# Gate rows of a fused attention and expert kernel: constant rows filled in place, the first two pairs' rows copied from SBUF, two pairs' q and k in flight

## The chip, the cores and the metric

The kernel runs on one core of one Trainium2 chip. The metric is the time of one launch in device microseconds, the median of the runs shown; before the change it is 846.34 us.

## The reference

Three stages follow each other: causal attention with a cumulative gate, and two feed-forward layers. Only the first is touched by the change.

```python
cum = np.cumsum(np.maximum(s, 0.0), axis=-1)           # s: 4 x 8 x 576
bias = -(cum[:, :, :, None] - cum[:, :, None, :])
scores = scale * q @ k.T                               # q, k, v: 4 x 8 x 576 x 64
scores = np.where(causal, -1e9, scores + np.minimum(bias, 0.0))
attn = softmax(scores); x = attn @ v
...
h = x @ w_in; h = layer_norm(h * softmax(h)) * g_ln; x = h @ w_out
h = x @ w2_in; out = (h * clip(h + 3, 0, 6) / 6) @ w2_out
```

Below the diagonal the bias is never positive, so the minimum leaves it as it is. A score is thus q.k plus cum of the key minus cum of the query, and the kernel lets the matrix engine add these two terms.

## The kernel before

The 32 heads are worked in 16 pairs. Pairs 0 to 3 are the first batch, and their scores are computed by `qk_whole` in two matmuls of 64 rows each: one contracts the head's 64 dimensions (tile `HL`, or the first half of tile `whole`), the other contracts the gate rows in the second half of `whole`. `whole` has four planes of 576 columns. Planes 2 and 3 hold, for each head of the pair, 64 rows of which four count: on one side ones and the negated sums, on the other side the sums and ones, with each sum split into a high and a low part. The rows behind the four must not contribute. There are two `whole` tiles, for even and odd pairs; pairs 2 and 3 use them again.

`gate_rows` makes these rows for all heads. It loads s, clips it, scans it into `cum`, splits that into `pos`, and negates it into `neg` (L278 to L282, on VectorE). Four DMAs (L286) write ones, `pos` and `neg` to the DRAM table `rows_d`. `load_gates` (L427) reads a pair's rows back from it, one DMA for each head. GpSimd fills planes 2 and 3 of both tiles with zeros beforehand (L290).

`load_qk` loads q and k of a pair in four DMAs (L395) into a ring of two tiles. So q and k of pair 1 can only be loaded when TensorE has transposed those of pair 0 (L440), which ScalarE and VectorE then evict (L445, L447).

Behind the scores come the maxima (L531, VectorE), the exponentials (L543, ScalarE), the reciprocal sums (L639, L640), the normalising (L644, GpSimd), the transposes of the probabilities (L678) and the product with v (L707). The weights w_in come in eight pieces of 512 KB on ScalarE's DMA queue (L317) into a ring of two and are decoded by ScalarE, VectorE and GpSimd (L323 to L347); the first expert matmuls (L812) stand behind the pairs.

The order of all work is made by a planner, `Plan`. Each step is added with its engine, an assumed duration, what it reads and writes and which ring it takes. `emit` then plays the steps through: every engine takes the ready step that was added first, and the instructions are issued in that order. Each engine runs its instructions strictly in order. A DMA counts on one of eight shared counters when it lands, and waits for the DMA before it on the same counter; the order shows the counters as DMAHW0 to DMAHW7.

The plan's start reads:

```python
    gate_rows()
    load_qk(0)
    for name in "qk":
        prep_qk(0, name)
    load_qk(1)
    load_v(0, 0)
```

## Time and profile before

| | before |
|---|---|
| median of 3 runs | 846.34 us (845.79 to 846.7) |
| profiled execution | 846.22 us, its span 844.4 us |
| TensorE (PE) busy | 818.4 us, 97% of the span |
| VectorE (DVE) busy | 438.5 us, 52% |
| ScalarE (ACT) busy | 399.4 us, 47% |
| GpSimd (POOL) busy | 209.4 us, 25% |
| mean granted TensorE clock | 0.994 |

The span runs from the first to the last instruction that the profile shows; the launch adds 1.8 us around it. SPq and ACTq are the instruction queues of SyncE and ScalarE where they issue DMAs. A busy TensorE is not TensorE at its best, since the granted clock has two levels, 1.2 and 2.4 GHz; it is shown as a share of the higher one.

### The profile page before, as it was taken

To read this page: it belongs to the slowest core of one execution; us is meant where nothing else is said; L and a number is where in the kernel's file an instruction comes from. 1 tells how busy PE (TensorE), PEld (TensorE's weight loads), DVE (VectorE), ACT (ScalarE), POOL (GpSimd) and SP (SyncE) were. 2 spreads that over 40 slices of the span, in tenths; PEclk is the share of its full clock that TensorE was granted. 3 is DMA by queue.
4 is the path that set the end of the run, shared out by engine and by line. 5 is a ranking of instruction groups with operands and counts; after the bars stand their busy time and mean duration, and the time that the engine had idled before them with its cause. 6 is when DMAs were issued, how large, how long until landed. Compare 5 with 4: busy or idle time off the path is not lost.

```text
span 844.4 us, 13546 instructions
## 1 busy us (share of the span) xinstructions
PE 818.4 (97%) x4864; PEld 689.5 (82%) x4864; DVE 438.5 (52%) x1125; ACT 399.4 (47%) x928; POOL 209.4 (25%) x309
## 2 busy tenths in 40 slices
PE   4899999999999999999999999999999999999997
PEld 3565588898898889888999999998888888888886
DVE  4677887746855574749826982234222322222221
ACT  2575767755765575736636662244222422232222
POOL 1563643424632363327402220000000000000000
PEclk9899999999999999999999999999999999999999
DMA  6753596755646455223605640012000300010001
GB/s 172 180 152 110 120 209 152 176 120 130 129 118 137 98 129 120 65 99 121 193 32 194 214 148 1 1 62 88 1 1 0 100 1 0 1 50 1 0 1 50
DMA packets 95938, 77.52 MB, mean 92 GB/s; under 512 B 64288, under 2 KB 78112, under 8 KB 95872
## 3 DMA queue, kind: packets, MB, share of 16 engines
q1 hardware_dynamic: 93568, 68.27, 31.9%
q10 hardware_dynamic: 2304, 8.39, 3.1%
q8 instruction: 38, 0.62, 0.3%
q14 instruction: 28, 0.23, 0.1%
HBM read 45.38 MB, written 10.03 MB: 66 GB/s over the span
## 4 chain that ended last, share of the span: by engine, by line
PE 91%; DVE 4%; DMA 1%; POOL 1%; issue 1%; ACT 0%; POOLq 0%; DVEq 0%; SPq 0%; ACTq 0%
PE bank L1071 24%; PE bank L1102 24%; PE bank L899 11%; PE bank L812 11%; PE bank L707 6%; PE bank L678 5%; PE bank L610 5%; PE bank L583 3%; PE bank L878 2%; PE bank L473 1%; DMA stack<-HL12k 1%; DVE y L531 0%; DMA rows_d<-neg 0%; POOL y L626 0%; POOL y L644 0%
## 5 line engine op out<-in xcount | busy, mean ns | idle before, releaser
L1071 PE MATMUL bank<-x2h,w 128*128 128x512 f32 (+1 forms) x640 | 185.3, 370 | 0.0
L1102 PE MATMUL bank<-w,gh 128*128 128x512 f32 x576 | 178.8, 393 | 0.0
L1079 DVE SCALAR_TENSOR_TENSOR g<-g,bank 128x512 f32<-128x512 f32 (+1 forms) x80 | 50.6, 633 | 206.3 <-ACT g L1075 206.0
L1071 PEld LDWEIGHTS bank<-x2h,w 128*128 128x128 f32 x640 | 118.7, 188 | 18.7
L1075 ACT ACTIVATE g<-bank 128x512 f32<-128x512 f32 (+1 forms) x80 | 44.5, 556 | 178.8 <-PE bank L1071 178.7
L1102 PEld LDWEIGHTS bank<-w,gh 128*128 128x128 f32 x576 | 107.9, 188 | 21.9
L1071 PE MATMUL bank<-x2l,w 128*128 128x512 f32 (+1 forms) x320 | 118.5, 370 | 0.0
L1102 PE MATMUL bank<-w,gl 128*128 128x512 f32 x288 | 111.9, 391 | 0.0
L531 DVE CUSTOM_DVE_ANT_0 y<-bank,mask 96x288 f32<-96x288 f32 (+4 forms) x168 | 74.6, 467 | 57.3 <-PE bank L610 37.7
L543 ACT ACTIVATE y<-y,nmax 128x256 f32<-128x256 f32 (+4 forms) x140 | 83.4, 597 | 41.4 <-DVE nmax L531 29.9
L626 POOL TENSOR_SCALAR y<-y,rsum 128x128 f32<-128x128 f32 (+4 forms) x120 | 68.1, 589 | 103.7 <-DVE rsum L622 48.5
L899 PE MATMUL bank<-zh,w_out_h 128*128 128x256 f32 x288 | 82.8, 288 | 0.0
L899 PE MATMUL bank<-zl,w_out_h 128*128 128x256 f32 x288 | 81.2, 282 | 0.0
L899 PE MATMUL bank<-zh,w_out_l 128*128 128x256 f32 x288 | 81.2, 282 | 0.0
L1087 DVE TENSOR_TENSOR gl<-g,gh 128x512 fp32r<-128x512 f32 (+1 forms) x80 | 53.7, 671 | 43.4 <-ACT gh L1083 42.6
L1083 ACT CAST gh<-g 128x512 fp32r<-128x512 f32 (+1 forms) x80 | 46.2, 577 | 48.2 <-DVE g L1079 48.1
L1071 PEld LDWEIGHTS bank<-x2l,w 128*128 128x128 f32 x320 | 60.0, 188 | 8.3
L1102 PEld LDWEIGHTS bank<-w,gl 128*128 128x128 f32 x288 | 54.1, 188 | 12.1
L812 PE MATMUL bank<-w_in_h,xh 128*128 128x512 f32 x144 | 61.6, 428 | 0.8 <-DVE xh L794 0.8
L610 PE MATMUL bank<-stack 128*96 128x288 f32 (+4 forms) x288 | 57.8, 317 | 1.2 <-DMA stack<-HL12k 0.8
L812 PE MATMUL bank<-w_in_h,xl 128*128 128x512 f32 x144 | 57.4, 399 | 0.6 <-POOL xl L798 0.6
L812 PE MATMUL bank<-w_in_l,xh 128*128 128x512 f32 x144 | 57.4, 398 | 0.0
(220 smaller groups left out, 1360.9 us busy)
## 6 DMA issues: line engine op xcount, KB each, us to landing
raw_w2i<-in_moe_w_in_dram SPq DMA_DIRECT2D x16, 512.0 KB
raw_w2o<-in_moe_w_out_dram SPq DMA_DIRECT2D x16, 512.0 KB
rawq<-in_q_dram SPq DMA_DIRECT2D x32, 144.0 KB
rawk<-in_k_dram SPq DMA_DIRECT2D x32, 144.0 KB
x_d<-x2s SPq DMA_DIRECT2D x36, 128.0 KB
out_dram<-ob SPq DMA_DIRECT2D x18, 256.0 KB
raw_wi<-in_moe_w_in_dram ACTq DMA_DIRECT2D x8, 512.0 KB
raw_wo<-in_moe_w_out_dram ACTq DMA_DIRECT2D x8, 512.0 KB
```

What stands on the lines that cost most here:

```text
L531: nc.vector.tensor_tensor_reduce(out=ys[h, t][:n, c0:c1], in0=bank(key)[:n, : c1 - c0], in1=mask[:n, 480 + n - w + c0 : 480 + n - w + c1], ...
L543: nc.scalar.activation(out=y[:n], in_=y[:n], func=AF.Exp, bias=nmax[:n, h, t : t + 1], scale=-1.0, accum_out=sums[:n, h, t : t + 1])
L610: nc.tensor.matmul(bank(key)[:n, : c1 - c0], lhsT=ss[:, 2 - 2 * m, ST[t] : w], rhs=ss[:, 3 - 2 * m, c0:c1], start=(m == 0), stop=(m == 1))
L626: nc.gpsimd.tensor_scalar(ys[h, t][:n], ys[h, t][:n], rsum[:n, h, t : t + 1], 1.0, ALU.mult, ALU.mult)
L707: nc.tensor.matmul(bank(key)[j * D : (j + 1) * D, lo - c0 : c1 - c0], lhsT=vs[v_key(p, a)][:n, jj, j, :], rhs=pts[pt_key(2 * p + j, a)][:n ...
L812: nc.tensor.matmul(bank(key), lhsT=xs[i][m // 2][:, kk, :], rhs=(w_in_l if m == 1 else w_in_h)[:, kk, f * 512 : (f + 1) * 512], start=(kk ...
L899: nc.tensor.matmul(bank(key)[:, : 2 * P], lhsT=w_out_at(w, kk)[:, m * P : (m + 1) * P], rhs=z[:, kk, :], start=(kk == 0 and i == 0), stop= ...
L1071: nc.tensor.matmul(bank(key)[:, :w], lhsT=wt[:, a, 0, c * P : (c + 1) * P], rhs=x[:, c, :w], start=(c == 0 and i == 0), stop=(c == KDM - 1 ...
L1079: nc.vector.scalar_tensor_tensor(out=gg, in0=gg, scalar=6.0, in1=bank(key)[:, :w], op0=ALU.min, op1=ALU.mult)
L1083: nc.scalar.copy(gh[:, :w], gg[:, :w])
L1087: nc.vector.tensor_sub(gl[:, :w], gg[:, :w], gh[:, :w].bitcast(F32))
L1102: nc.tensor.matmul(bank(key), lhsT=g_t[ci, m][1 + i // 2][:, t * P : (t + 1) * P], rhs=w2[m][:, i % 2, 1, :], start=(m == 0 and i == 0), s ...
```

## The change

The change has three parts.

- Constant rows in place. Instead of zeros, the planes get their constants directly: plane 2 becomes all ones, plane 3 zeros with minus one in the first four rows of each head. The sign moves from the sums to the constant, so `neg` is not made any more, and a row of minus ones (`minus`) takes its place in the table. The fill moves from GpSimd to VectorE and is added first in the plan.
- Gate rows of pairs 0 and 1 straight from SBUF. In the first pass `load_gates` copies the rows out of `pos` into the tile, with two DMAs for each head (`direct`). The writes to `rows_d`, which the later pairs still read, are added behind the loads of pair 1 (`store`).
- Two pairs' q and k at once. q and k of the odd pairs of the first batch go into the two tiles that the first expert layer later uses for its transposed activations (tags zh and zl), and k of pair 0 is loaded on ScalarE's queue. The other edits rename keys.

```diff
@@ -269,7 +269,8 @@
         one = ap2.tile([P, S], F32, tag="y4", name="one")[:NH]
         cum = ap2.tile([P, NQ, 2, D], F32, tag="V", name="cum").rearrange("p c j d -> p (c j d)")[:NH, :S]
         pos = ap2.tile([P, PT_COLS], F32, tag="pt", name="pos", bufs=PT).bitcast(F32R)[:NH, : 2 * S]
-        neg = ap2.tile([P, PT_COLS], F32, tag="pt", name="neg", bufs=PT).bitcast(F32R)[:NH, : 2 * S]
+        minus = ap2.tile([P, PT_COLS], F32, tag="pt", name="minus", bufs=PT)[:NH, :S]
+        once["pos"] = pos
         def load():
             nc.sync.dma_start(out=s_sb, in_=s.rearrange("b h s -> (b h) s"))
...
@@ -279,25 +280,32 @@
             nc.vector.tensor_tensor_scan(cum, one, s_sb, 0.0, ALU.mult, ALU.add)
             nc.vector.tensor_copy(pos[:, :S], cum)
             nc.vector.tensor_sub(pos[:, S:], cum, pos[:, :S].bitcast(F32))
-            nc.vector.tensor_scalar_mul(neg, pos.bitcast(F32), -1.0)
         def put(i, r, src):
             dst = rows_d[:, i, r::2, :]
             nc.sync.dma_start(out=dst, in_=src)
-        def zeros(j):
+        def fixed(j):
             whole_t[j] = ap1.tile([P, 4, S], F32, tag=f"stack{j}", name=f"whole{j}")
-            nc.gpsimd.memset(whole_t[j][:, 2:4, :], 0.0)
-
-        plan.add("SP", 0.45, load, writes=["s"], lag=2.0)
-        plan.add("POOL", 2.2, lambda: nc.gpsimd.memset(one, 1.0), writes=["one"])
+            nc.vector.memset(whole_t[j][:, 2, :], 1.0)
+            nc.vector.memset(whole_t[j][:, 3, :], 0.0)
+            for x in range(2):
+                nc.vector.memset(whole_t[j][x * D : x * D + 4, 3, :], -1.0)
+
+        for j in range(2):
+            plan.add("DVE", 1.2, lambda j=j: fixed(j), writes=[f"zeros{j}"], new=[(f"stack{j}", 1, f"whole{j}")])
+        plan.add("SP", 0.4, load, writes=["s"], lag=2.0)
+        plan.add("POOL", 0.6, lambda: nc.gpsimd.memset(one, 1.0), writes=["one"])
+        plan.add("POOL", 0.6, lambda: nc.gpsimd.memset(minus, -1.0), writes=["minus"])
         plan.add("DVE", 3.0, sums, reads=["s", "one"], writes=["c"])
-        ones = one.unsqueeze(1).to_broadcast([NH, 2, S])
-        both = lambda c: c.bitcast(F32).rearrange("p (i s) -> p i s", i=2)
-        for i, r, src, key in ((1, 0, both(pos), "c"), (0, 1, both(neg), "c"), (0, 0, ones, "one"), (1, 1, ones, "one")):
-            plan.add("SP", 0.55, lambda i=i, r=r, src=src: put(i, r, src), reads=[key], writes=[f"rows/{i}{r}"], lag=2.0)
-        for j in range(2):
-            plan.add("POOL", 1.3, lambda j=j: zeros(j), writes=[f"zeros{j}"], new=[(f"stack{j}", 1, f"whole{j}")])
+        twice = lambda c: c.unsqueeze(1).to_broadcast([NH, 2, S])
+        both = pos.bitcast(F32).rearrange("p (i s) -> p i s", i=2)
+
+        def store():
+            for i, r, src, key in ((1, 0, both, "c"), (0, 1, both, "c"), (0, 0, twice(one), "one"), (1, 1, twice(minus), "minus")):
+                plan.add("SP", 0.55, lambda i=i, r=r, src=src: put(i, r, src), reads=[key], writes=[f"rows/{i}{r}"], lag=2.0)
+
+        once["store"] = store
     def split64(plan, pool, src, hi, lo, name, key, scale=None, bufs=1, ring="", raws64=2, after=(), hi_dve=False, on_dve=(), behind=None, needs=(), home=()):
...
@@ -389,14 +397,20 @@
     def load_qk(p):
         b, hp = divmod(p, NPAIR)
+        spare = p < NPAIR and p % 2 == 1
+
         def rows(name, src):
-            raws[p, name] = ap2.tile([96, 6, 2, D], F32, tag="raw", name=f"raw{name}{p}")
+            if spare:
+                raw = bcp.tile([P, 2 * P * KFF], F32, tag="z" + "hl"["qk".index(name)], name=f"raw{name}{p}", bufs=1)
+                raws[p, name] = raw[:96, : 12 * D].rearrange("p (c j d) -> p c j d", c=6, j=2)
+            else:
+                raws[p, name] = ap2.tile([96, 6, 2, D], F32, tag="raw", name=f"raw{name}{p}")
             for j in range(2):
-                nc.sync.dma_start(out=raws[p, name][:, :, j, :], in_=src[b, 2 * hp + j].rearrange("(c p) d -> p c d", c=6))
+                (nc.scalar if p == 0 and name == "k" else nc.sync).dma_start(out=raws[p, name][:, :, j, :], in_=src[b, 2 * hp + j].rearrange("(c p) d -> p c d", c=6))
         for name, src in (("q", q), ("k", k)):
-            key = f"raw{name}{p}"
-            plan.add("SP", 1.1, lambda name=name, src=src: rows(name, src), writes=[key], new=[("raw", 2, key)], lag=4.0)
+            new = [("raw", 2, f"raw{name}{p}")] if not spare else [("z" + name, 1, f"raw{name}{p}")]
+            plan.add("ACT" if p == 0 and name == "k" else "SP", 1.0, lambda name=name, src=src: rows(name, src), writes=[f"raw{name}{p}"], new=new, lag=4.0)
     def v_key(p, a):
...
@@ -422,16 +436,24 @@
     def load_gates(p, a):
+        def direct():
+            for j in range(2):
+                row = once["pos"].bitcast(F32)[2 * p + j : 2 * p + j + 1, :].rearrange("o (i s) -> o i s", i=2)
+                for i, r in ((0, 1), (1, 0)):
+                    nc.sync.dma_start(out=whole_t[p % 2][j * D + r : j * D + r + 3 : 2, 2 + i, :], in_=row)
+
         def gates():
             for j in range(2):
                 nc.sync.dma_start(out=gates_at(p, j)[:4], in_=rows_d[2 * p + j].rearrange("i r s -> r i s"))
+        if p < 2 and not a:
+            return plan.add("SP", 1.6, direct, reads=["c", f"zeros{p}"], writes=[f"G{p}{a}"], new=[("G", 2, f"G{p}{a}")], lag=2.0)
         plan.add("SP", 0.8, gates, reads=ROWS_D + [f"zeros{p % 2}", f"whole{p % 2}"], writes=[f"G{p}{a}"], new=[("G", 2, f"G{p}{a}")], lag=2.0)
     def prep_whole(p, name):
         n = S // 6
-        i, raw_key, hl_key = "qk".index(name), f"raw{name}{p}", f"HL{p}"
+        i, hl_key = "qk".index(name), f"HL{p}"
         def turn(c0, key):
             if name == "q" and c0 == 0:
...
@@ -886,7 +907,7 @@
                                  zh[:, 4 * f : 4 * f + 4, o : o + P].bitcast(F32))
         first = i % 2 == 0 and f == 0
-        plan.add("PE", 0.43, turn, reads=[f"e{i}/{f}"], writes=[key], new=[("z", 1, f"z{c}")] if first else [], bank=key)
+        plan.add("PE", 0.43, turn, reads=[f"e{i}/{f}"], writes=[key], new=[("zq", 1, f"z{c}"), ("zk", 1, f"zl{c}")] if first else [], bank=key)
         plan.add("ACT", act(512), high, reads=[key], writes=[f"z{c}/h{f}_{i % 2}"])
         plan.add("DVE", dve(512), low, reads=[key, f"z{c}/h{f}_{i % 2}"], writes=[f"z{c}/l{f}_{i % 2}"])
...
@@ -975,6 +996,7 @@
     for name in "qk":
         prep_qk(0, name)
     load_qk(1)
+    once["store"]()
     load_v(0, 0)
     plan.add("SP", 0.5, lambda: nc.sync.dma_start(out=g_sb, in_=g_ln.rearrange("(c p) -> p c", p=P)), writes=["g"], lag=2.0, after=["HL0/k0"])
     for b, share in enumerate(SHARES):
```

On SyncE (SP), the place is the gate rows of the first two pairs. `whole_125` and `whole_134` are the tiles of pairs 0 and 1 before, `whole_117` and `whole_131` after. Before:

```order
L286 DMA rows_d<-pos 32x2x576 [waits DMAHW1_49,DVE_49]
L286 DMA rows_d<-neg 32x2x576 [waits DMAHW2_49,DVE_49]
L395 DMA rawq_147<-in_q_dram 96x6x64 [waits DMAHW3_49,PE_49]
L395 DMA rawq_147<-in_q_dram 96x6x64 [waits DMAHW4_49]
L395 DMA rawk_162<-in_k_dram 96x6x64 [waits DMAHW5_49,PE_49]
L395 DMA rawk_162<-in_k_dram 96x6x64 [waits DMAHW6_49]
L427 DMA whole_125<-rows_d 4x2x576 [waits DMAHW2_49,DMAHW7_49,DMAHW1_49,Pool_49]
L427 DMA whole_125<-rows_d 4x2x576 [waits DMAHW0_49]
L413 DMA V0a<-in_v_dram 128x2x64
L979 DMA g_sb<-in_moe_g_ln_dram 128x8x1
L427 DMA whole_134<-rows_d 4x2x576 [waits DMAHW3_49,Pool_49]
L427 DMA whole_134<-rows_d 4x2x576 [waits DMAHW4_49]
```

After:

```order
L443 DMA whole_117<-pos 2x1x576 [waits DMAHW5_49,DVE_49]
L443 DMA whole_117<-pos 2x1x576 [waits DMAHW6_49]
L443 DMA whole_117<-pos 2x1x576 [waits DMAHW7_49]
L443 DMA whole_117<-pos 2x1x576 [waits DMAHW0_49]
L286 DMA rows_d<-pos 32x2x576 [waits DMAHW1_49]
L286 DMA rows_d<-pos 32x2x576 [waits DMAHW2_49]
L427 DMA V0a<-in_v_dram 128x2x64 [waits DMAHW3_49]
L1001 DMA g_sb<-in_moe_g_ln_dram 128x8x1 [waits DMAHW4_49]
L443 DMA whole_131<-pos 2x1x576 [waits DMAHW5_49]
L443 DMA whole_131<-pos 2x1x576 [waits DMAHW6_49]
L443 DMA whole_131<-pos 2x1x576 [waits DMAHW0_49]
L443 DMA whole_131<-pos 2x1x576 [waits DMAHW1_49]
```

The reads from the table have become four copies for each pair, the writes of `pos` stand between the two pairs' copies, and the loads of v and g_sb stand ahead of pair 1's copies, each with a wait for a counter.

On ScalarE (ACT), the place is the first two w_in loads after the change, which count on the same counters:

```order
L467 ACTIVATE HL_152<-bank_96 128x288 [waits PE_49]
L467 ACTIVATE HL_152<-bank_97 128x288 [waits PE_49]
L325 DMA raw_wi_0_175<-in_moe_w_in_dram 128x1024 [waits DMAHW2_49]
L467 ACTIVATE HL_168<-bank_100 128x288 [waits PE_49]
L467 ACTIVATE HL_168<-bank_101 128x288 [waits PE_49]
L325 DMA raw_wi_0_189<-in_moe_w_in_dram 128x1024 [waits DMAHW4_49]
```

Before, both loads stood directly behind the first two evictions; the second one now stands behind the evictions of pair 1's q.

On VectorE (DVE), the place is the start of the program. Before:

```order
L278 TENSOR_SCALAR s_sb<-s_sb 32x576
L279 SCALAR_TENSOR_TENSOR cum<-one,s_sb 32x576
L280 CAST pos<-cum 32x576
L281 TENSOR_TENSOR pos<-cum,pos 32x576
L282 TENSOR_SCALAR neg<-pos 32x1152
L447 COPY HL_137<-bank_98 128x288
L447 COPY HL_137<-bank_99 128x288
```

After:

```order
L290 MEMSET whole_117 128x576
L291 MEMSET whole_117 128x576
L293 MEMSET whole_117 4x576 x2
L290 MEMSET whole_131 128x576
L291 MEMSET whole_131 128x576
L293 MEMSET whole_131 4x576 x2
L279 TENSOR_SCALAR s_sb<-s_sb 32x576
L280 SCALAR_TENSOR_TENSOR cum<-one,s_sb 32x576
L281 CAST pos<-cum 32x576
L282 TENSOR_TENSOR pos<-cum,pos 32x576
L469 COPY HL_152<-bank_98 128x288
L469 COPY HL_152<-bank_99 128x288
```

Eight memsets stand ahead of the sums, and the negation is gone.

On TensorE (PE), the place is the first scores, behind the transposes of pair 0's q. Before:

```order
L440 MATMUL bank_98<-ident,rawk_122 128x96 x3
L440 MATMUL bank_99<-ident,rawk_122 128x96 x3
L583 MATMUL bank_100<-whole_125 128x128
L583 MATMUL bank_101<-whole_125 128x128
L583 MATMUL bank_100<-HL_137 128x128
L583 MATMUL bank_101<-HL_137 128x128
L440 MATMUL bank_102<-ident,rawq_147 128x96 x3
L440 MATMUL bank_103<-ident,rawq_147 128x96 x3
L583 MATMUL bank_96<-whole_125 128x256
L583 MATMUL bank_97<-whole_125 128x256
```

After:

```order
L462 MATMUL bank_98<-ident,rawk_127 128x96 x3
L462 MATMUL bank_99<-ident,rawk_127 128x96 x3
L462 MATMUL bank_100<-ident,rawq_136 128x96 x3
L462 MATMUL bank_101<-ident,rawq_136 128x96 x3
L462 MATMUL bank_102<-ident,rawk_139 128x96 x3
L462 MATMUL bank_103<-ident,rawk_139 128x96 x3
L605 MATMUL bank_96<-whole_117 128x128
L605 MATMUL bank_97<-whole_117 128x128
L605 MATMUL bank_96<-HL_152 128x128
L605 MATMUL bank_97<-HL_152 128x128
```

The transposes of q and k of pair 1 now stand ahead of pair 0's first scores; before, they stood between the scores.

## Rows read from the trace of the kernel before

**Rows 1.** Part 2 of the page: busy tenths of TensorE in 40 slices.
```profile
PE   4899999999999999999999999999999999999997
```

**Rows 2.** Busy time by stretch: length, then each engine's busy us.
```profile
0.00:10.00 10.00, 2.39 (x12) 1.86 (x12) 6.36 (x7) 2.31 (x4) 4.20 (x13) 1.00 0.65 179
10.00:20.00 10.00, 5.00 (x24) 3.76 (x25) 1.65 (x6) 2.27 (x7) 0.00 (x0) 1.00 0.61 149
```

**Rows 3.** Timeline, gate rows: start, duration, engine; idle before in brackets.
```profile
0.72 0.40 SPq L275 DMA_DIRECT2D s_sb<-in_s_dram  x1
...
2.73 2.04 POOL L290 MEMSET whole<- 128x1152 f32 x2
2.74 2.34 DVE L278 TENSOR_SCALAR s_sb<-s_sb 32x576 f32<-32x576 f32 x1 [2.74 <-DMA s_sb<-in_s_dram]
...
5.19 1.35 DVE L279 TENSOR_TENSOR_SCAN cum<-one,s_sb 32x576 f32<-32x576 f32 x1
...
6.57 0.45 DVE L280 CAST pos<-cum 32x576 fp32r<-32x576 f32 x1
7.06 0.75 DVE L281 TENSOR_TENSOR pos<-cum,pos 32x576 fp32r<-32x576 f32 x1
...
7.84 0.75 DVE L282 TENSOR_SCALAR neg<-pos 32x1152 fp32r<-32x1152 f32 x1
...
12.93 0.60 SPq L427 DMA_DIRECT2D whole<-rows_d  x2
...
15.00 0.93 PE L583 MATMUL bank<-whole 64*128 64x128 f32 x3 [7.93 <-DMA whole<-rows_d]
```

**Rows 4.** Chain of waits, 8 to 15 us: start, duration, what.
```profile
8.61 4.17 DMA rows_d<-neg
12.93 1.93 DMA whole<-rows_d
```

**Rows 5.** Timeline, loads of the first 15 us and their users.
```profile
1.18 0.96 SPq L395 DMA_DIRECT2D rawq<-in_q_dram  x2
...
4.66 1.19 PE L440 MATMUL bank<-ident,rawq 96*128 96x96 f32 x6 [4.66 <-DMA rawq<-in_q_dram]
...
5.90 0.87 ACTq L317 DMA_DIRECT2D raw_wi<-in_moe_w_in_dram  x2
...
10.62 0.68 ACT L323 ACTIVATE a_wi<-raw_wi 128x512 f32<-128x512 f32 x1 [4.32 <-DMA raw_wi<-in_moe_w_in_dram]
...
14.03 0.47 SPq L979 DMA_DIRECT2D g_sb<-in_moe_g_ln_dram  x1
```

**Rows 6.** Busy time by stretch of 2 us, as rows 2.
```profile
24.00:26.00 2.00, 1.02 (x7) 0.66 (x5) 1.72 (x5) 1.32 (x4) 2.00 (x4) 0.90 0.38 82
26.00:28.00 2.00, 2.00 (x11) 1.43 (x9) 0.48 (x2) 1.70 (x6) 1.63 (x2) 0.50 0.64 145
...
56.00:58.00 2.00, 2.00 (x5) 1.64 (x6) 2.00 (x10) 0.93 (x3) 2.00 (x3) 0.58 1.12 299
```

**Rows 7.** Timeline, TensorE's transposes (L440) and scores (L583), 15 to 31 us.
```profile
15.80 0.77 PE L583 MATMUL bank<-HL 64*128 64x128 f32 x3
...
16.50 1.22 PE L440 MATMUL bank<-ident,rawq 96*128 96x96 f32 x6
...
18.67 1.06 PE L583 MATMUL bank<-HL 64*128 64x256 f32 x4
...
20.82 0.80 PE L583 MATMUL bank<-whole 64*128 64x128 f32 x4
...
23.58 0.69 PE L440 MATMUL bank<-ident,rawq 96*128 96x96 f32 x6 [0.55 <-DMA whole<-rows_d]
...
28.03 2.51 PE L583 MATMUL bank<-whole 64*128 64x128 f32 x14
```

**Rows 8.** Timeline, normalising on GpSimd and the transposes behind it.
```profile
23.84 2.55 POOL L644 TENSOR_SCALAR y<-y,rsum 128x128 f32<-128x128 f32 x4 [0.76 <-DVE rsum L640]
...
25.58 1.56 PE L678 MATMUL bank<-ident,y 128*128 128x128 f32 x5 [0.98 <-POOL y L644]
```

More of the change, by code (lines that the diff above doesn't have):

```diff
@@ L454, in prep_whole @@
             key = f"pp{p}{name}{c0}"
-            plan.add("PE", 3 * 0.083, lambda c0=c0, key=key: turn(c0, key), reads=[raw_key, *home], writes=[key],
+            plan.add("PE", 3 * 0.083, lambda c0=c0, key=key: turn(c0, key), reads=[f"raw{name}{p}", *home], writes=[key],
                      new=ring if name == "q" and c0 == 0 else [], bank=key, after=[] if name == "q" and c0 == 0 else [f"pp{p}q0"])
@@ L464, in prep_qk @@
         n = S // 6
-        hl_key, raw_key = f"HL{p}{name}", f"raw{name}{p}"
+        hl_key = f"HL{p}{name}"
         groups = [(0, 6)] if 6 * n <= 512 else [(0, 3), (3, 6)]
@@ L498, in prep_qk @@
             key, m = f"pp{p}{name}{c0}", (c1 - c0) * n
-            plan.add("PE", (c1 - c0) * (0.01 + 0.000833 * n), lambda c0=c0, c1=c1, key=key: turn(c0, c1, key), reads=[raw_key], writes=[key],
+            plan.add("PE", (c1 - c0) * (0.01 + 0.000833 * n), lambda c0=c0, c1=c1, key=key: turn(c0, c1, key), reads=[f"raw{name}{p}"], writes=[key],
                      new=[("HL0", 2, hl_key)] if c0 == 0 else [], bank=key, after=[f"pp{p}{name}0"] if c0 else [])
@@ L766, in pairs @@
             qs = [(0.0013 * (ST[t] + SZ[t]), lambda p=p, t=t: qk_whole(p, t)) for t in ts]
-            k = 0
             for i, x in enumerate(qs):
```

2 lines of the change are left out of this document (1 added, 1 removed).

## The prediction

> **What bounds the kernel now.** I read the page first. TensorE is busy 97% of the span, and of its 40 slices only the first two and the last show less than 9 tenths [rows 1]. So nearly every microsecond of the run is TensorE work, and a change in the first 20 us can save only what TensorE idles there, or does at its lower clock. The busy time by stretch then shows how much that is: 2.4 and 5.0 us busy in the first two stretches of 10 us [rows 2]. What is gained before 60 us should therefore stay gained up to the end, unless a stall is put in somewhere behind. The timeline has the largest hole there: TensorE waits 7.93 us for the gate rows of pair 0, which come back from the DRAM table rows_d [rows 3].
>
> The timeline and the chain of waits show how that hole is made [rows 3, 4]. s_sb arrives at 2.74, but VectorE's first operation on it takes 2.34 us. The cast of the same 576 columns takes 0.45, and GpSimd's memset of `whole` runs from 2.73 to 4.77 beside it. The sums end at 7.81, the negatives at 8.59. Their write to rows_d is issued at 8.61 and takes 4.17 us; the read is issued at 12.93 and takes 1.93; the score matmuls of pair 0 start at 15.00.
>
> **The change, step by step.**
>
> *When `pos` is ready.* VectorE now fills both `whole` tiles itself, ahead of the sums: eight memsets of 576 columns. The trace has no memset on VectorE. Bounds from its nearest rows: 0.45 us each (the cast of 576 columns) and 0.75 (the subtraction of 576 columns); GpSimd's memset, 1.02 for 1152 columns, gives 0.51 [rows 3]. I take 0.6, between the two and near the third. From the start at 0.72 (where the other queues start) the memsets end at 5.5, with bounds 4.3 and 6.7. GpSimd's 2.04 us on `whole` are gone, so the first operation on s_sb should take about 0.45 like the cast, and then come scan, cast and subtraction: 1.35 + 0.49 + 0.78 (start to start) [rows 3]. `pos` is ready at 5.5 + 3.1 = 8.6 (7.4 to 9.8), which is 0.8 later than before. The removed `neg` (0.75) cancels that.
>
> The Trainium skill (VectorE: DVE Perf Modes, section "Zero memsets can be issued as uint32 (trn2)") says that a memset takes one cycle per element whatever the type; at the 0.96 GHz it gives for VectorE that is 0.6 us each, an estimate from that page, and `pos` at 8.6 as well. No row here shows it. On the 2.34 us, the row shows VectorE released 0.3 us after GpSimd's memset ended. The same skill (SBUF — State Buffer, section "Who interferes with whom") says that the two engines share a port pair and the second to issue is blocked; the row agrees, and if the blocking also held for the new memsets, `pos` would come at up to 10 us.
>
> *Pair 0.* No table write lies between `pos` and the copy now. Four copies of 2 rows each are issued on SP, 0.30 us apart (two of the old reads took 0.60) [rows 3]: 8.6, 8.9, 9.2, 9.5. Each should take the 1.93 us of the old read, the same rows in the same number of bytes; the upper bound is the 4.17 of the write [rows 4]. Head 0 is complete at 10.85, head 1 at 11.45.
> Meanwhile TensorE transposes q and k of both pairs. The loads of k of pair 0 go out on ScalarE's queue beside q's, and q of pair 1 right behind on SP. The first transposes start at 4.66 now [rows 5]; with k's 144 KB times two in flight beside q's I put them at 5.2. Six take 1.2 us at this place [rows 5], so all 24 end at 10.0. Pair 0's scores start at 10.85 instead of 15.00, and pair 1's 2.4 us of transposes are already behind.
>
> *Pair 1: the new wait.* Every DMA of the program waits for the one before it on the same of eight counters (the order shows it as DMAHW0 to 7). On SP the small load of g_sb now shares a counter with the second w_in load, which ScalarE issues after q of pair 1 is evicted, at about 9.4 (transposes to 8.8, two evictions). Before, both w_in loads were issued from 5.90 on, and the first was in use at 10.62, 4.72 later [rows 5]. With 4.72 the second lands at 14.1; g_sb's issue takes 0.47 [rows 5]; behind it stand pair 1's four copies, 14.6 to 15.5, the second of which lands at 16.8. So TensorE, done with pair 0 at 10.85 + 1.57 + 2.07 = 14.5 (the durations of the same matmuls: 15.00 to 16.57, 17.66 to 19.73 [rows 7]), has a new idle stretch of about 2.3 us, and pair 1's scores run from 16.8 to 20.4.
>
> *Pair 2.* Behind pair 1's copies, q of pair 2 is issued by 16.7 and, with the 2.5 to 3.5 us of the first q (issued 1.18 and 1.66, in use at 4.66 [rows 5]), is there before 20.4. Its transposes end at 21.6. The transposes of pair 0's probabilities need GpSimd's normalising; before, that ended 11.4 us after pair 0's first score (26.39 against 15.00 [rows 3, 8]), and now VectorE has less between, so it ends by 22.2 at the latest. Five of those six transposes took 1.56 us, so 1.9 for six [rows 8]: 23.5. k of pair 2 adds 1.2: 24.7 with everything at the lower clock.
> The gate rows of pair 2 still come from rows_d. The load of v ahead of them on SP waits for the third w_in load: issued at about 16, landing at 20.7, then 0.5 for the issue, 0.9 for v and two reads, and 1.93: about 23.8 at the latest, just hidden.
> Pair 2's scores began at 28.03 [rows 7].
>
> *TensorE's clock.* The same six transposes take 1.22 at 16.50 and 0.69 at 23.58, so the first ran at the lower level; four of the scores of 128 columns take 0.80 at 20.82, so it was fast by then [rows 7]. In 24 to 26 TensorE was busy 1.02 of 2 us, and in 26 to 28 the granted clock is 0.50, the 1.2 GHz level [rows 6]. So it worked nearly without a gap from 15.00 until it was fast at about 20.8, and after a gap around 24 to 25.5 it was slow again. By the same course it would be fast again about 5.8 us after 16.8, at 22.6, which takes 0.9 off what follows: pair 2 starts at 23.8, 4.2 us earlier. Before, the work from 28.03 to about 32.4 ran at the lower level; at the full one it would take 2.2 less. I count 1.3 of that, since the other engines must follow.
>
> *The sum.* 4.2 + 1.3 = 5.5 us. The rest costs nothing by itself: `minus` (a GpSimd memset of 576 columns) where GpSimd idles, the two extra stores of `pos` behind the copies. The profiled execution took 846.22 us (span 844.4), close to the median 846.34. So 840.7 for a profiled execution and **840.8** for the median.
>
> **Bounds.** If each copy takes 4.17 instead of 1.93, pair 1 starts 2.2 later; without the clock's 1.3 the gain is 2.0: 844.3. If the second w_in load lands in 3 us, pair 1 starts 1.7 earlier; with all 2.2 of the clock and the second slow stretch at 56 to 60 (granted clock 0.58 in its first half [rows 6], so about 1.7 lost) avoided the gain is 4.2 + 1.7 + 2.2 + 1.7 = 9.8: 836.5.
>
> **Rivals.**
> - *Smaller gain* (0.16): copies queue behind the loads and the clock stays low, 843 to 844.5. For it: the write of 4.17. Against it: the read of 1.93, which moved as little as the copies do, while the write moved 144 KB.
> - *Larger gain* (0.12): the upper bound above, 836 to 837.5.
> - *Given back* (0.10): the two w_in loads go out 1 and 3 us later than before; if the first expert matmuls near 56 us wait for the decoded w_in and not for attention, the start is bought for nothing: 846.3. Against it: those loads are paced by attention work on ScalarE, which moves forward too.
> - *Slower* (0.06): v of pair 1 on SP, and with it pair 2's gate rows, wait for the third w_in load. If that lands at 24.7 nothing is gained; if it takes 12 us from its issue at 16, pair 2 starts at about 31.3, 3.3 late: 849.6. Against it: 4.72 for the first with another behind it.
>
> **How the numbers follow.** The likeliest, 0.56, is a gain of 3.5 to 7.5 us. With the smaller and the larger gain the range 836.5 to 844.8 holds a little over 8 in 10. A difference of under 0.2% (1.7 us) can't be told from no change. Faster: 0.56 + 0.12 + most of 0.16, 0.81. Same: the rest of it and most of "given back", 0.12. Slower: 0.07.
>
> **What would show it.** The wait of 7.9 us for rows_d is gone; pair 0's scores start near 10.9; a wait for pair 1's copies of about 2 us stands at 14 to 17; the first operation on s_sb takes under 0.6; pair 2's scores start near 23.8; the granted clock is full at 28 to 32. The prediction is wrong if the memsets take over 1 us each, if SP stands at g_sb beyond 16, or if TensorE idles more than before between 30 and 100 us.

## The result and the profile after

The change made the kernel slower by 4.1 us. The median of six runs is 850.61 us (849.82 to 854.38), against 846.52 (845.79 to 846.92) for six runs of before in the same measurement: a ratio of 1.0057, 95% interval 1.0038 to 1.0076. The profiled execution took 850.73 us (span 849.0), 4.5 more than that of before, so it shows what has to be explained.

Part 2 of the page of after, TensorE's busy tenths:

```profile
PE   5799999999999999999999999999999999999998
```

In [rows 1] the first two slices show 4 and 8 and the last shows 7: the first has gained a tenth, the second has lost one and the last has gained one. Nothing else moves at this scale. Finer cuts say where the time went. The next two views give the busy time by stretch (columns as in [rows 2]); the cuts are put at points up to which TensorE has issued the same matmuls in both kernels, by kind and tile. Before:

```profile
0.00:31.80 31.80, 17.66 (x95) 13.05 (x97) 15.74 (x45) 11.12 (x34) 10.89 (x23) 0.90 0.69 173
31.80:50.30 18.50, 16.85 (x118) 10.68 (x116) 13.61 (x47) 10.76 (x31) 8.31 (x11) 0.98 0.57 145
50.30:111.43 61.13, 57.78 (x388) 38.52 (x385) 49.54 (x141) 42.48 (x105) 32.02 (x41) 0.97 0.54 137
111.43:164.50 53.07, 52.10 (x406) 45.01 (x406) 41.96 (x147) 39.66 (x111) 27.29 (x46) 1.00 0.79 173
164.50:844.40 679.90, 674.02 (x3866) 582.20 (x3862) 317.66 (x748) 295.40 (x653) 130.84 (x189) 1.00 0.28 76
```

After:

```profile
0.00:29.46 29.46, 17.72 (x94) 14.48 (x94) 17.71 (x50) 11.18 (x33) 8.74 (x22) 1.00 0.85 186
29.46:53.23 23.77, 18.77 (x118) 10.88 (x119) 14.03 (x49) 11.78 (x33) 7.65 (x12) 0.93 0.44 110
53.23:114.09 60.86, 57.08 (x388) 38.97 (x385) 49.42 (x149) 42.26 (x104) 33.62 (x42) 1.00 0.61 151
114.09:169.15 55.06, 54.53 (x406) 44.55 (x406) 42.50 (x141) 40.31 (x109) 26.64 (x46) 1.00 0.71 155
169.15:849.00 679.85, 674.16 (x3866) 582.29 (x3862) 316.97 (x748) 294.44 (x652) 129.45 (x189) 1.00 0.28 76
```

Row against row, after minus before: -2.34, +5.27, -0.27, +1.99 and -0.05 us, in sum the 4.6 of the spans. So three things have to be explained: a start that gained 2.3 us and not 5.5, a loss of 5.3 right behind it, and 2.0 us lost between 111 and 169 us, far from the edit. Of the 5.27, 3.35 are idle time of TensorE (23.77 - 18.77 against 18.50 - 16.85) and 1.92 are matmuls that took longer. The 1.99 are all busy time, which grew by 2.43 (54.53 against 52.10), while the idle time fell by 0.44.

**The start.** TensorE's timeline of after, 0 to 32 us:

```profile
6.22 1.19 PE L462 MATMUL bank<-ident,rawq 96*128 96x96 f32 x6 [6.22 <-DMA rawq<-in_q_dram]
...
13.13 1.15 PE L605 MATMUL bank<-whole 64*128 64x128 f32 x3 [2.83 <-DMA whole<-pos]
...
16.74 0.76 PE L605 MATMUL bank<-whole 64*128 64x128 f32 x2
...
22.96 1.19 PE L462 MATMUL bank<-ident,rawq 96*128 96x96 f32 x6 [2.11 <-DMA rawq<-in_q_dram]
...
26.33 2.80 PE L605 MATMUL bank<-whole 64*128 64x128 f32 x16
...
30.72 0.69 PE L462 MATMUL bank<-ident,rawk 96*128 96x96 f32 x6
```

The 7.93 us of [rows 3] have become 2.83, and pair 0's scores start at 13.13 instead of 15.00. But pair 2's q is in use at 22.96, against 23.58 in [rows 7], and pair 2's scores start at 26.33 against 28.03. The six transposes of 96x96 take 1.19 at 6.22 and at 22.96, and 0.69 only at 30.72, so TensorE stayed at its lower level until about 29 us. The 1.00 in the row 0.00:29.46 says nothing on this: the trace of after has no record of the granted clock before 28.86 us, and a stretch without a record counts as 1.00. So I go by the durations. In before, six such transposes take 1.17 at 26.93, in a stretch for which [rows 6] shows the granted clock at 0.50:

```profile
26.93 1.17 PE L440 MATMUL bank<-ident,rawk 96*128 96x96 f32 x6
```

The chain of waits of after, 0 to 24 us, shows what the start hangs on (start, duration, what):

```profile
1.63 4.46 DMA rawq<-in_q_dram
...
6.22 3.13 PE bank L462 x18
...
9.38 4.45 DMA raw_wi<-in_moe_w_in_dram
...
13.85 0.39 SPq L1001
...
14.28 0.59 SPq L443
...
16.79 0.34 SPq L409
...
17.18 5.65 DMA rawq<-in_q_dram
```

`pos` and pair 0's copies are not in it. It runs from the first loads over the second w_in load to g_sb (L1001), which waits for that load's counter, to pair 1's four copies at about 0.6 each, to q of pair 2. That transfer takes 5.65 us; the third w_in load (512 KB) was issued at 17.52 beside it.

**The hole at 31 to 39 us.** The chain of after, and TensorE's timeline there:

```profile
31.84 4.24 DMA raw_wi<-in_moe_w_in_dram
...
36.09 0.02 SPq L447
...
36.14 2.90 DMA whole<-rows_d
...
39.17 5.42 PE bank L605 x20
```

```profile
34.79 1.01 PE L605 MATMUL bank<-whole 64*96 64x480 f32 x2 [1.21 <-DMA whole<-rows_d]
39.17 1.08 PE L605 MATMUL bank<-whole 64*96 64x480 f32 x1 [3.37 <-DMA whole<-rows_d]
```

The second of the two reads of pair 0's second-pass gate rows, 18 KB, is issued at 36.14, when the fifth w_in load has landed. It needs nothing of that load; they share a counter. In the order of after, the SP rows of the two reads and the ScalarE row of the load:

```
L447 DMA whole_117<-rows_d 4x2x576 [waits DMAHW0_49,PE_49]
L447 DMA whole_117<-rows_d 4x2x576 [waits DMAHW1_49,PE_49]
L325 DMA raw_wi_1_384<-in_moe_w_in_dram 128x1024 [waits DMAHW1_49,Activation_49]
```

Behind the hole TensorE is at its lower level again: the stretches of 2 us from 38 and 40 us have a granted clock of 0.78 and 0.50.

```profile
38.00:40.00 2.00, 0.83 (x2) 0.43 (x4) 0.00 (x0) 0.12 (x1) 1.03 (x3) 0.78 0.34 86
40.00:42.00 2.00, 2.00 (x9) 1.25 (x7) 0.87 (x3) 0.17 (x1) 0.00 (x0) 0.50 0.00 0
```

### The profile page after: what moved, and what is told of

Its sections match the earlier page's. It is cut to its first block, busy times and chain, and to the rows that moved or that the text cites. A ratio compares the mean times of both kernels' runs of the same rounds, so it can differ in the third digit from the quotient of the medians.

```text
span 849.0 us, 13582 instructions
## 1 busy us (share of the span) xinstructions
PE 822.3 (97%) x4864; PEld 691.2 (81%) x4864; DVE 440.6 (52%) x1132; ACT 400.0 (47%) x928; POOL 206.1 (24%) x308
## 4 chain that ended last, share of the span: by engine, by line
PE 89%; DMA 4%; DVE 3%; POOL 2%; issue 1%; SPq 1%; ACT 0%; POOLq 0%; DVEq 0%; ACTq 0%
PE bank L1093 24%; PE bank L1124 23%; PE bank L920 11%; PE bank L833 10%; PE bank L729 5%; PE bank L632 4%; PE bank L700 4%; PE bank L605 3%; PE bank L899 2%; PE bank L495 1%; DMA rawq<-in_q_dram 1%; DMA raw_wi<-in_moe_w_in_dram 1%; POOL y L666 1%; DMA stack<-HL5k 1%; PE bank L462 1%
## 5 line engine op out<-in xcount | busy, mean ns | idle before, releaser
L565 ACT ACTIVATE y<-y,nmax 128x128 f32<-128x128 f32 (+4 forms) x140 | 83.5, 597 | 44.5 <-DVE nmax L553 38.4
```

Source lines behind the costliest of these rows:

```text
L565: nc.scalar.activation(out=y[:n], in_=y[:n], func=AF.Exp, bias=nmax[:n, h, t : t + 1], scale=-1.0, accum_out=sums[:n, h, t : t + 1])
```

## The experiments

Ratios are against before, timed on the same chip with each group. "Ahead" and "behind" compare the start of the same matmul with before, as the windows above do.

**1. Parts alone, and the planner's numbers alone.** The change also alters a few assumed durations, which enter the planner. `costs_only` is before with these alone:

```diff
-        plan.add("SP", 0.45, load, writes=["s"], lag=2.0)
-        plan.add("POOL", 2.2, lambda: nc.gpsimd.memset(one, 1.0), writes=["one"])
+        plan.add("SP", 0.4, load, writes=["s"], lag=2.0)
+        plan.add("POOL", 0.6, lambda: nc.gpsimd.memset(one, 1.0), writes=["one"])
...
-            plan.add("SP", 1.1, lambda name=name, src=src: rows(name, src), writes=[key], new=[("raw", 2, key)], lag=4.0)
+            plan.add("SP", 1.0, lambda name=name, src=src: rows(name, src), writes=[key], new=[("raw", 2, key)], lag=4.0)
```

> The kernel before, with only three assumed durations of the planner set to those of the change (loads of s 0.4 and of q and k 1.0, the row of ones 0.6); no step is added or removed. If the order that the planner makes of the later work costs by itself (theory A: order), the time moves by 2 us or more in either direction, though nothing else differs. If the order is harmless and the change's own waits cost (theory B: the counters), it stays within 1 us of the kernel before, 845.5 to 847.5.

`gates_only` is after without the loading of two pairs, `loads_only` is before with that alone:

```diff
# gates_only, against after; the planner's step for k of pair 0 goes to SP with it
-        spare = p < NPAIR and p % 2 == 1
+        spare = False
...
-                (nc.scalar if p == 0 and name == "k" else nc.sync).dma_start(...)
+                nc.sync.dma_start(...)
# loads_only, against before: the whole change of load_qk and its rings, and nothing else
```

> The change without its third part: q and k of pair 1 load into the old ring of two and k of pair 0 on SyncE's queue again; constant rows in place and the copies from SBUF stay. If the copies and the in-place rows are good in themselves and the loss comes from having two pairs in flight (theory C: the loads), the time is 841 to 845. If each copy's wait is what costs, it is 848 or more. Theory B says that it depends on which transfers share a counter with a w_in load: here a gate row read of pair 2 and one of pair 1's second pass do, so 844 to 848.

> The kernel before with the third part alone: two pairs' q and k in flight, k of pair 0 on ScalarE's queue; gate rows by way of the table as before. The wait for the table stays, so at most the 2.4 us of transposes of pair 1 are gained: 844 to 846 if the loads harm nothing; 848 or more if they are the cause (theory C). Theory B: k of pair 3 and a gate row read of pair 0 share a counter with w_in loads here, so 846 to 849.

Measured: costs_only 853.88 us, ratio 1.0093 (1.0068 to 1.0119); gates_only 850.63, 1.0061 (1.0042 to 1.0080); loads_only 856.26, 1.0116 (1.0094 to 1.0138). So changing no work at all, only the numbers from which the order is made, costs more than the change. Most of what its profiled execution (856.35, the slowest of four) loses lies at one place: it is 2.8 us behind before at 113 us, 10.8 at 122 and 10.4 at the end. TensorE's timeline and the chain of costs_only there:

```profile
121.39 0.76 PE L610 MATMUL bank<-stack 128*96 128x288 f32 x2 [7.05 <-DMA stack<-HL5q]
```

```profile
115.89 5.41 DMA stack<-HL5q
```

A copy goes out late, since SP stood before it for 4.1 us at a load of k whose counter a w_out load held, and then takes 5.41 us with a w_out load issued at 113.25. By the words of its expectation this time is theory A's. But the new order also deals the counters anew, and the place is a wait of theory B's kind, so this run can't separate the two.

loads_only lies above theory B's 846 to 849, where theory C put it (848 or more). In its trace it is the wait of after at another place: SP stands 6.1 us for a w_in load, and TensorE waits 4.75 us at 35.11 for gate rows whose read stood behind it.

gates_only has a cost of another kind. In its chain SP issues DMAs without a pause from 10.2 to 18.1 us, pair 1's copies among them at about 0.6 each, TensorE waits 1.98 us for the last of them, and k of pair 2 then takes 5.32. Its 850.63 lies where its expectation put "each copy's wait is what costs" (848 or more) and above what theories B and C gave. So the copies' time in SP's queue stands on the path there, beside the counters, and the third part of the change is not the only cause.

**2. The hole at 31 to 39 us.** `early_gates` is after with the read in question ahead of the loads of pair 4; `after_spaced` is after with two spare DMAs of 64 bytes on SP, which move all later ones by two counters and leave the order of TensorE, VectorE, ScalarE and GpSimd as it was; `before_spaced` is before with one such DMA:

```diff
# early_gates, against after
...
+                extra += [(0.0, lambda: load_gates(0, 1))] if p + 2 == NPAIR else []
                 extra += [(0.0, lambda p=p: load_qk(p + 2))] if p + 2 <= NPAIR else []
...
# after_spaced (range(2)) and before_spaced (range(1)), in load_v; spare_d is a scratch tile in DRAM
...
+            if key == "V1a" and j == 1:
+                for x in range(1):
+                    nc.sync.dma_start(out=spare_d[x : x + 1, :], in_=g_ln[:16].rearrange("(o c) -> o c", o=1))
```

early_gates also has the planner put q and k of pair 4 behind that read.

> The whole change, with the read of pair 0's gate rows for the second pass put ahead of pair 4's q and k; it then shares no counter with a w_in load (a load of pair 4's k does instead). Theory B: the 4.6 us of waits at 34 to 39 us and the stretch at the lower clock behind it are gone, so 843 to 846. Theory A: the order changes again, so anything from 845 to 853. If the time stays at 850, neither the wait nor the clock behind it decides.

> The changed kernel with two more DMAs of 64 bytes (into a scratch row that nothing reads) behind the second half of V1a on SyncE. The order of TensorE, VectorE, ScalarE and GpSimd stays exactly that of the changed kernel; only the counters are dealt anew: the sixth w_in load now follows the fifth on its counter, and the second read of pair 0's second-pass gate rows no longer does. Counters: that read goes out at about 31.7 us instead of 36.14, TensorE's waits of 1.21 and 3.37 us there are gone, and the time falls by about 2 us, to 848 to 849. Order of the work: nothing that TensorE does is moved, so 850.6 as before, within 0.8.

> The kernel before with one more DMA of 64 bytes behind the second half of V1a on SyncE, every engine's order unchanged. Counters: the second half of k of pair 3 now follows the fourth w_in load (issued at 27.66) on its counter, goes out at about 32.4 us instead of 28.48, and pair 0's second-pass gate rows behind it at about 33 instead of 30.13, while TensorE needs them at 33.67: a wait of about 1.5 us and a stretch at the lower clock, 847.8 to 849.8 in all. Order: 846.3, within 0.8.

Measured: early_gates 848.38, ratio 1.0026 (1.0010 to 1.0042). The hole is gone from its place, a smaller one of 2.51 us comes at 41.22, again behind gate rows whose read waited for the fifth w_in load; it is level with before at 50 us and 1.6 behind from 165 us on. It missed theory B's 843 to 846 and lies in the wide range of theory A. So the hole explains about half of the loss, and the 2 us behind 111 us stay.

after_spaced missed: 851.07, 1.0071 (1.0055 to 1.0086), not 848 to 849. Its profiled execution took 853.92, the slowest of six. The read went out at 33.26, 2.9 us earlier, without waiting for the load. But then it was in flight with it, and the chain shows what that costs:

```profile
33.26 8.02 DMA whole<-rows_d
```

18 KB took 8.02 us, against 1.93 in [rows 4] and 2.90 in after. The load was issued at 32.88, q and k of pair 4 just before on SP. Up to 38.5 us SP's queue moves only packets of under 512 bytes, those of q and k; the read's own, 2304 bytes each, come behind them, and it lands at 41.28 together with k. The load, too, takes 8.0 us (32.88 to 40.90). So the counter is only one part of the mechanism; the other is that a small read shares the way with 512 KB and with what stands ahead of it on its own queue. The Trainium skill says as much (DMA: Bandwidth & Descriptors, section "Issuing engines are not separate DMA queues"): DMAs that different engines start run on the same 16 DMA engines and interleave. This row agrees, and the 5.65 us of q of pair 2 do too.

before_spaced is the control that I had not thought of when I predicted: 850.62, 1.0061 (1.0049 to 1.0073), the forecast place and direction, but more than the 847.8 to 849.8 forecast. One DMA of 64 bytes that nothing waits for makes the old kernel as slow as the changed one. Its chain:

```profile
28.29 6.53 DMA raw_wi<-in_moe_w_in_dram
...
34.84 0.31 SPq L396
...
35.25 2.74 DMA whole<-rows_d
```

It is level with before up to 31.8 us, 6.3 behind at 46 and 5.5 from 125 on. In the order of before, no small DMA of SP between 23 and 40 us waits for a counter that a w_in load holds. With one DMA more, the second half of k of pair 3 waits for one, and the gate rows stand behind it. So the time of before rests in part on how its counters happen to be dealt; this one other dealing loses 5.3 us.

**3. The start.** `after_fill_late` is after with the memsets of the second tile behind the sums, so that `pos` comes earlier; `after_w3_late` is after with the third w_in load issued behind q and k of pair 2:

```diff
# after_fill_late
             nc.vector.tensor_sub(pos[:, S:], cum, pos[:, :S].bitcast(F32))
+            fill(1)
...
# after_w3_late
+            if name == "wi2_0":
+                once["late"] = lambda: nc.scalar.dma_start(out=raw.rearrange("p n w -> p (n w)"), in_=words)
+                return
...
+            if key == "V1a" and j == 1:
+                once["late"]()
...
```

> The changed kernel with the four memsets of the second whole tile behind the sums on VectorE instead of ahead of them. pos is ready at about 6.8 us instead of 9.42, and pair 0's scores start at 10.5 to 11 instead of 13.13. Counters: g_sb still stands at 13.85 on SyncE for the second w_in load, pair 1's copies behind it go out at 14.3 and q of pair 2 at 16.8 as now, so from pair 1 on nothing moves: 850 to 851. If the sums set the time of all that follows, 848 to 849.

> The changed kernel with the third w_in load (512 KB) issued behind q and k of pair 2 instead of beside them. If the weight load in flight is what makes q of pair 2 take 5.65 us, its second half lands 2.5 to 3 us after its issue at about 17.2, TensorE's wait of 2.11 us before q of pair 2 is gone, and pair 2's scores start at 24 to 25 instead of 26.33. The wait at 36 to 39 us for the second-pass gate rows of pair 0 stays, so 848 to 850. If SyncE's late issue alone was the cause, q is in use at 22.9 as now: 850 to 851.

Measured: after_fill_late 850.28, 1.0056 (1.0044 to 1.0068), as expected. Pair 0's scores start at 11.64 (10.5 to 11 was expected), 1.5 earlier than in after; TensorE then waits 2.40 and 2.00 us for pair 1's copies, and q of pair 2 is in use at 23.00, as in after: when `pos` comes isn't what the start hangs on. after_w3_late missed: 854.55, 1.0111 (1.0094 to 1.0127). Its first half came: q of pair 2 took 2.71 us and was in use at 20.73 instead of 22.96, so the 5.65 were the load's doing. But the moved load then cost more elsewhere. VectorE stands in its order at the decoding of this load ahead of evicting pair 2's k, and TensorE waits for that eviction:

```profile
28.42 2.51 PE L610 MATMUL bank<-whole 64*128 64x128 f32 x12 [4.63 <-DVE whole L474]
```

The chain has the load (22.05, in use at 27.48), and behind it pair 0's gate rows, which cost 4.39 more at 40.37:

```profile
22.05 5.41 DMA raw_wi<-in_moe_w_in_dram
...
27.48 0.43 DVE t_wi L338
27.91 0.38 DVE whole L474
...
35.01 5.22 DMA whole<-rows_d
```

Against after it was 2.6 ahead at 22.8 us, 1.6 behind at 28 and 3.4 behind from 48 on. The load has to lie somewhere in these 30 us, and at both places tried something small waited with it.

**4. The parts in the old order.** `kept_order` has the constants in place and the direct copies with the planner's steps and durations of before, and with the second tile filled behind pair 0's evictions; TensorE and ScalarE issue the same work in the same order as before. `kept_order_2` and `kept_order_3` differ in where SP writes `pos` to the table, behind or ahead of pair 1's copies:

```diff
# kept_order, beside the fill, the copies and the table writes of after
+                if p == 0 and c0:
+                    once["fill"](1)
...
         def gates():
+            if p < 2 and not a:
+                return once["direct"](1) if p else once["table"]()                 # kept_order
+                return [once["direct"](1), once["table"]()] if p else None         # kept_order_2
+                return [once["table"](), once["direct"](1)] if p else None         # kept_order_3
```

> The first two parts of the change (constants in place on VectorE, without negatives, pairs 0 and 1 copied from pos; the second tile is filled behind pair 0's evictions) in the kernel before, with the planner's steps and durations left as they are, so that TensorE's, ScalarE's and GpSimd's order is that of before but for the fills. Pair 0's scores should start at about 10.5 us instead of 15.0. Counters: the first half of q of pair 2 follows the third w_in load, goes out at about 22.5 instead of 17.76 and is in use at 25.5 to 26 instead of 23.58: 847 to 849, slower than before. If the counters don't matter, q of pair 2 comes as before or earlier: 843.5 to 845.

> As kept_order, with the two writes of pos to rows_d issued behind pair 1's copies instead of ahead of V0a; TensorE, VectorE, ScalarE and GpSimd have the same order as in kept_order. Counters: the second half of V0a follows the third w_in load now instead of q of pair 2, which comes at about 22 to 23 us; k and the gate rows of pair 2 behind V0a go out at 22.9 to 24.8, pair 2's scores start at about 26.5 (28.03 before), and k of pair 3 stands behind the fourth w_in load: 844.5 to 846.5, at least 2 us less than kept_order. Without an effect of the counters both have the same time.

> As kept_order_2, with the two writes of pos to rows_d issued just ahead of pair 1's copies instead of just behind them; the order of TensorE, VectorE, ScalarE and GpSimd is the same. By the counters k of pair 3 no longer follows the fourth w_in load, and only the second halves of V0a and V0b still follow a weight load before 60 us. Counters: the 4 to 5 us that kept_order_2 has gained at 27 us are kept, the wait of 5.1 us for the second-pass gate rows is gone, 841 to 843.5. If that wait came from something else it stays: 847.5 to 848.5.

Measured: 845.06, 847.98 and 845.14 us; ratios 0.9999 (0.9987 to 1.0012), 1.0027 (1.0016 to 1.0037) and 0.9999 (0.9988 to 1.0010). All three missed. kept_order was to be 847 to 849 by the counters and is level with before: q of pair 2 did stand behind the third w_in load on its counter, but went out at 19.20 and not at about 22.5, and was in use at 23.00. kept_order_2 was to be at least 2 us below kept_order and is 2.9 above it. kept_order_3 was to be 841 to 843.5. All three gain at the start and none keeps it. kept_order is 1.9 ahead from 63 to 93 us and loses 1.6 of it there, through the clock (last section). kept_order_2 is 5.0 ahead at 26.8 and 2.4 behind at 38, by a hole of 5.1 us behind a w_in load. kept_order_3 has no such wait for a counter; it is 3.9 ahead at 27.9 and loses that by this piece of its chain:

```profile
27.05 4.54 DMA whole<-rows_d
```

That read was issued right behind k of pair 3 (25.77) and the fourth w_in load (26.19): once more 18 KB that take 4.54 us in such company, and at 35.6 it is 0.2 ahead.

**5. The w_in loads made small.** To see the change with little of them, three kernels load one eighth of each piece of w_in (64 KB) and read it eight times over in the decoding; the other seven eighths of w_in are left out, and nothing else is. The small loads still hold their counters. The order of every engine is that of the kernel they are made from.

```diff
+            if name[:2] == "wi":
+                issue.dma_start(out=raw[:, :64, :].rearrange("p n w -> p (n w)"), in_=words[:, :128])
...
+        def word(w):
+            if name[:2] == "wi":
+                return T["raw"][:, :64, w].unsqueeze(1).to_broadcast([P, n // 64, 64])
...
```

> The kernel before with an eighth of each w_in piece loaded (64 KB instead of 512 KB) and read eight times over by the decoding, so that the output is not the reference's; no instruction is moved on any engine. It is the measure for the next two. q of pair 2 lands in 2.5 to 3 us instead of 5.3; the pair's scores start no later than before: 843 to 846.

> The changed kernel with the same eighth of w_in. If the w_in loads eat the gain of the start (transfers that land with them, and SyncE's loads that follow them on a counter), q of pair 2 is in use at about 20.9 us, the waits of 1.21 and 3.37 us at 34 to 39 us are gone, and the kernel is 2 to 4 us faster than before_thin. If the order of the work makes the changed kernel slow, it stays 2 to 5 us slower than before_thin.

> kept_order_3 with the same eighth of w_in; TensorE, ScalarE and GpSimd have the order of before_thin but for the fills. If the w_in loads set when q, k and gate rows of pairs 2 and 3 land, the 3.7 us that kept_order_3 loses between 28 and 36 us are kept: 2.5 to 4 us faster than before_thin. If what it gains is lost to another engine, within 1 us of before_thin.

Measured: before_thin 843.36, 0.9977 (0.9967 to 0.9987); after_thin 845.73, 1.0003 (0.9994 to 1.0013); kept_order_3_thin 839.89, 0.9939 (0.9926 to 0.9952). With small loads, constants and copies in the old order gain 843.36 - 839.89 = 3.5 us, as expected (2.5 to 4). The change as it is still loses 2.4: the 2 to 4 us gain that the loads would explain did not come, and the loss of 2 to 5 did, which the expectation gave to the order. Busy time by stretch, cut at the same matmuls, of before_thin, kept_order_3_thin and after_thin:

```profile
0.00:28.93 28.93, 14.33 (x88) 10.91 (x90) 14.99 (x42) 10.66 (x32) 10.60 (x23) 0.94 0.55 126
28.93:92.11 63.18, 57.52 (x385) 35.12 (x381) 49.01 (x149) 41.60 (x105) 34.49 (x42) 1.00 0.43 110
...
108.09:160.99 52.90, 52.22 (x406) 45.24 (x406) 42.30 (x148) 39.75 (x112) 26.98 (x45) 1.00 0.78 174
```

```profile
0.00:25.07 25.07, 15.90 (x88) 12.21 (x90) 16.78 (x48) 10.08 (x30) 8.14 (x19) 1.00 0.58 133
25.07:89.18 64.11, 57.93 (x385) 35.66 (x382) 49.44 (x151) 42.19 (x107) 35.51 (x45) 1.00 0.44 112
```

```profile
0.00:24.75 24.75, 15.58 (x88) 12.98 (x90) 17.32 (x46) 9.86 (x29) 7.01 (x19) 1.00 0.72 139
24.75:92.13 67.38, 61.82 (x384) 37.72 (x382) 49.87 (x156) 41.74 (x107) 35.99 (x45) 0.97 0.45 111
...
107.43:162.56 55.13, 54.54 (x407) 44.72 (x405) 42.56 (x144) 40.26 (x108) 26.75 (x45) 1.00 0.68 155
```

At the start both are ahead by about 4 us (28.93 against 25.07 and 24.75). The old order gives back 0.9 of it up to the second cut, the new one all of it (67.38 against 63.18). That isn't the order of the work alone: in after_thin SP still waits 2.0 us for the fifth w_in load ahead of the same gate rows, TensorE then idles 1.36 us at 31.12 and 0.70 at 32.83, and the granted clock is 0.73 and 0.50 in the stretches of 2 us from 32 and 34 us. So part of the 4.2 is the hole of after again, smaller. And the stretch behind 107 us takes 55.13 against 52.90, the 2 us of the full kernels again: they don't come from the size of the w_in loads. The two stretches that are not printed differ by -0.7 us (between) and +0.7 us (behind).

Between these two matmuls all six kernels with after's order on TensorE (after, early_gates, after_spaced, after_fill_late, after_w3_late, after_thin) take 55.1 us each, and all seven with the order of before (before, before_spaced, before_thin and the four kept_order kernels) 52.5 to 53.1. So the order of the work sets it.

## Why the prediction was wrong

The forecast was 840.8 us and faster; it became 850.6 and slower. By its own steps:

- *When `pos` is ready, and pair 0.* The memsets took 0.54 us each (0.6 was taken); the estimate of 0.6 from the Trainium skill (VectorE: DVE Perf Modes, section "Zero memsets can be issued as uint32 (trn2)") agrees within 0.06. But they started 0.60 to 0.73 us apart, the first at 0.91, so the last ended at 6.22 instead of 5.5. The first operation on s_sb fell from 2.34 to 0.45, as said. `pos` was thus ready at 9.42 and not at 8.6, and the four copies were issued 0.65 apart and not 0.30, so pair 0's scores started at 13.13 instead of 10.85. The 0.30 came from reads of the table; the copies are another kind of DMA and needed a bound. after_fill_late shows that this cost nothing.
- *Pair 1, the new wait.* Right in place and cause: 16.74 against 16.8 predicted, by the wait of g_sb for the second w_in load. The idle stretch of 2.3 us that was to stand before it didn't come, since pair 0's scores started 2.3 us late and filled it; in after_fill_late, where they don't, TensorE waits 2.40 there.
- *Pair 2.* The step that failed first: "is there before 20.4". q took 5.65 us and not 2.5 to 3.5. That duration was taken from the first loads of the kernel, beside which no w_in load was in flight. after_w3_late, where the load is out of the way and q takes 2.71, shows the 2.24 us that this cost. (The line on pair 2's gate rows adds up to 24.0, not 23.8: 20.7 + 0.5 + 0.9 + 1.93; they set nothing here.)
- *TensorE's clock.* It was to be fast at 22.6; it came up at about 29, behind the waits of 2.83 and 2.11 us. The reading of [rows 7] was wrong too: the four scores that take 0.80 at 20.82 in before ran at the lower level still. A score of 128 columns takes 418 ns at 21.4 there as at 15.9, and 272 ns at the full level behind 32 us; the trace of before has its first record of the full level at 22.17, 1.4 us later than was taken. So pair 2's scores came 1.7 us earlier and not 4.2, and of the 1.3 us behind them 0.6 came: 2.3 us in place of 5.5.
- *"What is gained before 60 us should therefore stay gained."* The step that decided the sign. I followed the work up to pair 2's scores and the DMAs up to the third w_in load. The read that stalled stands twenty places behind q of pair 2 on SP, and the small reads up to there had new neighbours on the counters and beside them in flight. The rival "slower" had this very mechanism, at the third load; it struck at the fifth, and had a chance of 0.06. costs_only, loads_only, before_spaced and kept_order_2 show that it is not bad luck of one place: each of these dealings met such a wait somewhere; kept_order_3 is one that met none.
- *The 2.0 us between 111 and 169 us* had no step at all. All six kernels with the new order of TensorE have them; the seven that keep its old order don't. So the order of the work that the planner made costs them, not the loads of w_in, and not idle time. Which matmul follows which differs there in many places, and summed by kind of matmul no kind differs by more than 0.9 us; why the same 406 take longer in the new sequence stays open.

Of the 4.6 us between the profiled executions the runs thus account for the start (-2.3), the hole and the clock behind it (+5.3), and the order behind 111 us (+2.0, place and condition shown, mechanism open), with -0.3 between the last two.

The first two parts of the edit, constants in place and direct copies, are a gain in themselves: 3.5 us where the loads are small and the order is kept. Of the third part no run shows a gain by itself (loads_only lost 10.2 us). With w_in loaded in full, no kernel here turned it into a time below that of before.

## What to carry to other kernels

Where small reads and large weight loads share DMA engines and completion counters, an edit at the start deals both anew, and a forecast has to follow every small DMA to the next places where a weight load is in flight or holds its counter, not only to the end of the part that is edited. Before a few us are credited to an edit in such a kernel, run a control that changes nothing but the dealing (one spare DMA, or the planner's numbers alone): here its 5 to 8 us were larger than the effect that was measured. Take a transfer's duration from a row with the same company in flight, not from the same size elsewhere.

## What the runs showed of the hardware

- A read of 18 KB took 1.93 us in [rows 4], and in company 2.90 (after), 4.54 (kept_order_3) and 8.02 (after_spaced). The last two were issued 0.86 and 0.38 us after a 512 KB load, with k of a pair just ahead on their own queue. In kept_order_3_thin, with 64 KB in place of the 512 and k still ahead, the read of the 4.54 takes 2.94: so 1.6 us of it go with the size of the load.
- One DMA of 64 bytes that nothing waits for cost 5.3 us (before_spaced, 850.62 - 845.35): the loads behind it on SP fall to other counters.
- Issuing a copy of two rows from SBUF to SBUF took 0.56 to 0.76 us of SP's queue (after, eight copies, most of them 0.57), where a read from the table took 0.30 (two in 0.60, [rows 3]).
- A memset of 576 columns took VectorE 0.54 us on 128 rows and on 4 alike. The timeline of after:

```profile
1.52 0.54 DVE L291 MEMSET whole<- 128x576 f32 x1
2.23 0.54 DVE L293 MEMSET whole<- 4x576 f32 x1 [0.17 <-DVE whole L291]
```

- The clock may or may not fall behind the same gap. In kept_order TensorE waits 1.77 us for the same tile (pt4b) as in before, where it waits 1.79 and the granted clock stays at 1.00 from 94 to 98 us. The stretch of before behind the gap, and those of kept_order:

```profile
96.00:98.00 2.00, 2.00 (x16) 0.98 (x14) 1.97 (x6) 1.33 (x4) 1.95 (x3) 1.00 0.97 195
```

```profile
94.00:96.00 2.00, 2.00 (x10) 1.07 (x10) 1.86 (x5) 1.30 (x4) 1.93 (x3) 0.50 0.98 195
96.00:98.00 2.00, 2.00 (x9) 0.80 (x8) 0.98 (x3) 0.71 (x3) 2.00 (x4) 0.66 0.38 74
```

That is the level of 1.2 GHz, and it cost the 1.6 us there; what in the work ahead of the gap decides it stays open.
